# Cached attention with a gated feed-forward branch: who begins the loads of keys and values

## The chip, the core and the metric

The kernel runs on one core of a Trainium2 chip. A core has a matrix engine (TensorE, PE in the profile), a vector engine (VectorE, DVE), a scalar engine (ScalarE, ACT), GpSimd (POOL) and SyncE (SP), which run their own instruction streams and meet at semaphores. Sixteen DMA engines move data between the chip's main memory (HBM) and the on-chip memory (SBUF); transfers are begun by an instruction on one of the engines' queues. The metric is the device time of one execution in microseconds (us), as the median of several runs.

## The reference, cut to what matters

```python
# x [4,1,512]; k_cache, v_cache [4,32,4096,128]; wq [512,4096]; wo [4096,512]
def _A_ref(x, k_cache, v_cache, wq, wo):
    q = (x @ wq).reshape(B, Sq, H, Dh).transpose(0, 2, 1, 3)
    scores = jnp.einsum("bhqd,bhkd->bhqk", q, k_cache) * (Dh ** -0.5)
    p = softmax(scores, axis=-1)
    o = jnp.einsum("bhqk,bhkd->bhqd", p, v_cache)
    return o.transpose(0, 2, 1, 3).reshape(B, Sq, H * Dh) @ wo

def _B_ref(x, w_gate, w_up, w_down):
    return (gelu(x @ w_gate) * (x @ w_up)) @ w_down

g = sigmoid((x * gate_w).sum(-1, keepdims=True))
out = g * _A_ref(...) + (1 - g) * _B_ref(...)
```

Everything is float32. The two caches hold 268 MB each, read once.

## The kernel before, in words

**Tiles.** A tile is four heads of one batch row: 8.39 MB of keys or of values, laid on 128 partitions with 64 KB in a row on each. There are 32 key tiles and 32 value tiles (NT = 32). Keys have two buffers, `K[0]` and `K[1]`, used in turn; values have one, `V`. The weights share these buffers: `wq` is loaded into `V` first, and `w_gate`, `w_up`, `w_down` and `wo` go into the key buffers at the end.

**The start.** SP begins `wq`, `x` and `gate_w` (L143 to L147), then key tiles 0 and 1 (L148, L149), all in one queue. GpSimd makes the identity matrix `ident` (L151, L153). TensorE turns `x` (L170), multiplies it with `wq` (L200) and turns the result (L212; its last mark is `wq_done`, after which `V` is free); ScalarE and TensorE spread the first query into `QB` (L225 to L231).

**One tile.** `keys(s)` on VectorE waits for the key tile (`sem_k[s]`) and for the query, multiplies in place (L293) and sums (L294); then it counts up `k_free`, which says that the key buffer may be filled again, and finds the maxima (L296 to L298). ScalarE takes exponentials (`weights`, L308). TensorE sums the weights (`totals`, L234), waits for the value tile (`sem_v`), multiplies (`values`, L241), and turns the result (`turn`, L246), whose first instruction gives the mark `at_tile[i]`: `V` is free again. VectorE divides (L301, L302).

**The order of the loads** (L338 to L344): SP waits for `wq_done` and begins value tile 0. Then, for i from 0 to 29, it waits for `k_free` to reach i + 1 and begins key tile i + 2, waits for `at_tile[i]` and begins value tile i + 1. Waits and loads stand in SP's program order, and each load (`load`, L132) is a `dma_start` on SP's queue that adds 16 to its semaphore when it has landed. The engines that use a tile subtract the 16 again (`take`, L122).

**The end** (L346 to L383): when key tile 30 is worked off, SP begins `w_gate` and `w_up` into `K[0]`, then value tile 31 (waiting for `at_tile[30]`), then, when key tile 31 is worked off, `w_down` and the first part of `wo` into `K[1]`. The products with `w_gate` and `w_up` (L280) run on TensorE in front of tile 31's; from them VectorE and ScalarE make `hT` (L362 to L375), and after it SP begins the rest of `wo` in five pieces. `project` (L401) adds the rows of `w_down` and `wo`; the last four rows of `wo` go through L456, and the result `res` (L460) is stored.

Of the kernel before, what the change touches and what calls it, by code (L numbers as in the profile page):

```python
# [34 lines left out]
def tile_gated_mix(ctx: ExitStack, tc: tile.TileContext, x, kc, vc, wq, wo, w_gate, w_up, w_down, gate_w, out):  # L35
    nc = tc.nc
# [10 lines left out]
    NT = NG * B  # L47
# [33 lines left out]
    K = [kv.tile([P, TW], F32, name=f"k{s}") for s in range(2)]  # L81
    V = kv.tile([P, TW], F32, name="v")
# [20 lines left out]
    tot, quo = bank[2][:, :HT], bank[3][:, :HT]  # L103

    stored, parting = (ctx.enter_context(nc.semaphore(name)) for name in ("stored", "parting"))
    counters = []

    def semaphore(name):
        counters.append(ctx.enter_context(nc.semaphore(name)))
        return counters[-1]  # L110

    ctx.enter_context(tc.tile_critical(sync_engine=mybir.EngineType.SP))
    SP = Line(nc.sync, None)
# [3 lines left out]
    PL = Line(nc.gpsimd, semaphore("pl"))  # L117
    a_to_p, d_to_p, p_to_a, d_to_a, p_to_d, a_to_d, d_to_d = (
        semaphore(name) for name in ("a_to_p", "d_to_p", "p_to_a", "d_to_a", "p_to_d", "a_to_d", "d_to_d"))
    k_free = semaphore("k_free")  # L120
# [4 lines left out]
    sem_k = [semaphore(f"sem_k{s}") for s in range(2)]  # L125
    sem_v = semaphore("sem_v")

    def heads(src, i):
        g, b = divmod(i, B)
        return src[b, HT * g:HT * g + HT].rearrange("h (p r) d -> (h p) (r d)", p=PH)  # L130

    def load(dst, src, sem=None, name=None):  # L132
        sem = sem or semaphore(name)
        nc.sync.dma_start(dst, src).then_inc(sem, 16)  # L134
        return sem, 16

    def load_k(i):
        load(K[i % 2], heads(kc, i), sem_k[i % 2])

    def load_v(i):  # L140
        load(V, heads(vc, i), sem_v)

    got_q = load(V, wq.rearrange("(p c) n -> p (c n)", c=KC), name="got_q")  # L143
    x_sb = o[:B]
    got_x = load(x_sb, x.rearrange("b s d -> (b s) d"), name="got_x")
    gw = gs[:B]
    got_g = load(gw, gate_w.rearrange("(o n) -> o n", o=1).to_broadcast([B, DM]), name="got_g")  # L147
    load_k(0)  # L148
    load_k(1)  # L149

    p0 = PL.do(nc.gpsimd.memset(ident, 0.0))  # L151
    PL.wait(p0)
    have_ident = PL.do(nc.gpsimd.affine_select(out=ident, in_=ident, compare_op=OP.not_equal, fill=1.0, base=0,  # L153
                                               pattern=[[-1, P]], channel_multiplier=1))
    DV.do(nc.vector.memset(ones, 1.0))
    DV.do(nc.vector.memset(PM, 0.0))
    have_zeros = DV.do(nc.vector.memset(RS, 0.0))
# [51 lines left out]
    for s in range(2):  # L209
# [3 lines left out]
        wq_done = PE.do(u)  # L213
# [43 lines left out]
    L1 = NT - 1  # L257
    PE.wait(have_QX, have_picks, have_zeros)
    at_tile = [(PE.sem, PE.n + i + 1) for i in range(NT)]
    f, down = K[0], K[1]  # L260
# [74 lines left out]
            beside(s, i)  # L335
    beside(0, None)

    SP.wait(wq_done)  # L338
    load_v(0)
    for i in range(NT - 2):  # L340
        SP.wait((k_free, i + 1))
        load_k(i + 2)
        SP.wait(at_tile[i])
        load_v(i + 1)  # L344

    wo_rows = wo.rearrange("(p i) n -> p (i n)", i=WR)  # L346
    SP.wait((k_free, NT - 1))
    for s, a in enumerate((w_gate, w_up)):
        load(f[:, s * KC * F:(s + 1) * KC * F], a.rearrange("(p c) n -> p (c n)", c=KC), sem_up[s])
    SP.wait(at_tile[L1 - 1])  # L350
    load_v(L1)
    SP.wait((k_free, NT))
    got_down = load(down[:, :DR * DM], w_down.rearrange("(p i) n -> p (i n)", i=DR), name="got_down")
    got_wo = [load(down[:, (DR + r0) * DM:(DR + r1) * DM], wo_rows[:, r0 * DM:r1 * DM], name=f"got_wo{r0}")
              for r0, r1 in ((0, W0), (W0, W1))]

# [88 lines left out]
    i = W2  # L445
# [15 lines left out]
    load(out.rearrange("b s (c n) -> c (b s) n", c=4), res[::8], stored)  # L461
    nc.sync.sem_inc(parting, 1)
    nc.gpsimd.wait_ge(parting, 1).then_inc(parting, -1)
    nc.gpsimd.sem_clear(range(counters[0].num, counters[-1].num + 1))
    nc.sync.wait_ge(stored, 16).then_inc(stored, -16)

# [21 lines left out]
```

## Time and profile before

| | |
|---|---|
| median of 3 runs | 1311.45 us (1311.39 to 1311.8) |
| profiled execution: span from first to last instruction | 1309.8 us |
| outside the span, against the median | 1.65 us |
| busy share of VectorE | 87% |
| busy share of TensorE, ScalarE, GpSimd | 30%, 8%, below 1% |
| HBM read | 564.67 MB, 431 GB/s over the span |

A time line row reads: start in us, duration in us, engine, line, operation, tile written and read, and in brackets the idle time before with what ended it. A row of costly groups has, after the count, the busy time in us, the mean of one in ns, and the idle time before them. A row of DMA issues has the tile, the queue, the count, the KB of one where they are few, and the median time from issue to landing in us. A row of a DMA queue has its packets, its MB and the share of the time of 16 engines. A row of the busy time by stretch has start and end, length, the busy us of PE, weight loads, DVE, ACT and POOL, the granted clock of TensorE, the DMA share and GB/s.

### The profile page before, as it was taken

How to read it: one execution, taken by the hardware profiler on the slowest of the kernel's cores; microseconds unless marked ns; L12 is line 12 of the kernel's file. 1: busy time of each engine (PE TensorE's matmuls, PEld its weight loads, DVE VectorE, ACT ScalarE, POOL GpSimd, SP SyncE). 2: the span in 40 equal slices, each digit the busy share in tenths (PEclk: the TensorE clock that was granted, in tenths of full speed). 3: DMA queues.
4: the chain of work that ended last, by engine and by line, in shares of the span. 5: the costliest groups of instructions: out<-in, count | busy, mean ns of one | idle time of the engine just before them, and what ended most of it. 6: DMA issues, size and time to landing. Idle time of an engine off the chain costs nothing. (4 is left out here: it accounts for less than half of the span.)

```text
span 1309.8 us, 6988 instructions
## 1 busy us (share of the span) xinstructions
PE 387.9 (30%) x2708; PEld 134.1 (10%) x2708; DVE 1144.5 (87%) x266; ACT 108.6 (8%) x360; POOL 0.7 (0%) x6
## 2 busy tenths in 40 slices
PE   2133123333213333312333321233231133332157
PEld 0010001111001111000111100011010011100012
DVE  1799999999999989989999998999999998999950
ACT  0000000000000000000000000000000000000010
POOL 0000000000000000000000000000000000000000
PEclk9665566666556666656666655666655666665578
DMA  9999999999999999999999999999999999999998
GB/s 417 416 445 421 444 432 432 444 422 442 424 442 422 444 438 426 444 424 442 422 442 428 438 442 424 442 424 442 422 444 432 432 444 422 442 424 442 423 433 352
DMA packets 10842, 564.76 MB, mean 431 GB/s; under 512 B 1212, under 2 KB 1228, under 8 KB 1620
## 3 DMA queue, kind: packets, MB, share of 16 engines
q1 hardware_dynamic: 10836, 564.69, 99.6%
q8 instruction: 3, 0.05, 0.0%
q14 instruction: 3, 0.02, 0.0%
HBM read 564.67 MB, written 0.01 MB: 431 GB/s over the span
## 5 line engine op out<-in xcount | busy, mean ns | idle before, releaser
L293 DVE TENSOR_TENSOR k<-k,QB 128x16384 f32<-128x16384 f32 x32 | 551.2, 17225 | 57.8 <-DVEq L123 57.8
L294 DVE TENSOR_REDUCE SC<-k 128x128 f32<-128x16384 f32 x32 | 551.0, 17220 | 4.7
L241 PE MATMUL bank<-v,PM 128*16 128x512 f32 x2048 | 292.8, 736 | 507.6 <-PEq L123 507.6
L241 PEld LDWEIGHTS bank<-v,PM 128*16 128x16 f32 x2048 | 68.8, 113 | 704.9 <-issue 704.8
L234 PE MATMUL bank<-RS,ones 128*128 128x4 f32 x64 | 17.9, 350 | 348.4 <-PEq L123 348.4
L308 ACT ACTIVATE PM<-SC,nm 32x128 f32<-32x128 f32 x128 | 66.0, 516 | 249.4 <-ACTq L123 247.9
L321 ACT ACTIVATE o<-bank 128x512 f32<-128x512 f32 x31 | 18.5, 597 | 811.7 <-ACTq L123 811.7
L234 PEld LDWEIGHTS bank<-RS,ones 128*128 128x128 f32 x64 | 16.0, 311 | 353.5 <-issue 353.5
L246 PE MATMUL bank<-pick,o 128*128 128x4 f32 x256 | 32.8, 252 | 28.8 <-PEq L123 28.8
L246 PEld LDWEIGHTS bank<-pick,o 128*128 128x128 f32 x256 | 31.0, 191 | 57.3 <-issue 57.3
L301 DVE RECIPROCAL ri<-bank 128x4 f32<-128x4 f32 x32 | 5.8, 183 | 22.5 <-DVEq L123 22.5
L308 ACT ACTIVATION_READ_ACCUMULATOR PM<-SC,nm 32x1 f32 x128 | 25.1, 196 | 0.0
L174 DVE COPY xT<-bank 128x32 f32<-128x32 f32 x4 | 0.5, 184 | 21.2 <-PE bank L170 21.2
L228 PE MATMUL bank<-ident,QX 128*128 128x128 f32 x66 | 15.5, 316 | 1.7 <-ACT QX L225 1.6
L296 DVE TENSOR_REDUCE m<-SC 128x1 f32<-128x128 f32 x32 | 9.2, 287 | 7.6 <-DVEq L123 7.6
L231 ACT ACTIVATE QB<-bank 128x128 f32<-128x128 f32 x32 | 8.9, 277 | 50.3 <-ACTq L123 49.7
L302 DVE TENSOR_TENSOR OT<-bank,ri 128x4 f32 (+1 forms) x32 | 5.2, 161 | 7.5 <-DVEq L123 7.2
L297 DVE STREAM_TRANSPOSE mt<-m 128x32 f32<-128x32 f32 x32 | 6.8, 211 | 4.7
L228 PEld LDWEIGHTS bank<-ident,QX 128*128 128x128 f32 x66 | 10.0, 191 | 3.2 <-issue 1.9
L460 DVE COPY res<-bank 128x128 f32<-128x128 f32 x1 | 0.3, 292 | 11.4 <-PE bank L456 11.4
L298 DVE TENSOR_REDUCE nm<-mt 128x1 f32<-128x32 f32 x32 | 6.0, 186 | 4.8 <-DVEq L123 2.1
L225 ACT ACTIVATE QX<-QT 128x128 f32 (+1 forms) x32 | 9.8, 308 | 2.4 <-DVE QT L216 1.6
(57 smaller groups left out, 61.1 us busy)
## 6 DMA issues: line engine op xcount, KB each, us to landing
k<-in_B_w_gate SPq DMA_DIRECT2D x1, 3584.0 KB, 31.3
k<-in_B_w_up SPq DMA_DIRECT2D x1, 3584.0 KB, 39.4
k<-in_B_w_down SPq DMA_DIRECT2D x1, 3584.0 KB, 29.0
k<-in_A_wo SPq DMA_DIRECT2D x1, 2560.0 KB, 34.7
k<-in_A_wo SPq DMA_DIRECT2D x1, 2048.0 KB, 39.1
k<-in_A_wo SPq DMA_DIRECT2D x1, 1536.0 KB, 33.6
k<-in_A_wo SPq DMA_DIRECT2D x1, 1024.0 KB, 35.7
k<-in_A_k_cache SPq DMA_DIRECT2D x32, 42.1
```

What stands on the lines that cost most here:

```text
L225: return nc.scalar.activation(QX, tile_of(QT, pair, s)[:, :, None].to_broadcast([P, HT, PH]), AF.Copy)
L228: return nc.tensor.matmul(qp[:, :D], QX.rearrange("p h k -> p (h k)"), ident, start=True, stop=True)
L231: nc.scalar.activation(QB[s], qp[:, :D], AF.Copy, scale=scale).then_inc(a_to_d, 1)
L234: return nc.tensor.matmul(tot, ones, RS, start=True, stop=True)
L241: t = nc.tensor.matmul(po[32 * c:32 * c + M], p[:, j * M:(j + 1) * M], V[:, j * RJ * D:(j + 1) * RJ * D], start=j < 4, stop=j >= n - 4)
L246: return [nc.tensor.matmul(quo, o[:, j * D:(j + 1) * D], pick[:, j, :], start=j == 0, stop=j == RJ - 1) for j in range(RJ)]
L293: then(nc.vector.tensor_tensor(k, k, QB[s][:, None, :].to_broadcast([P, R, D]), op=OP.mult))
L294: then(nc.vector.tensor_reduce(SC[s], k, axis=AX.X, op=OP.add))
L296: then(nc.vector.tensor_reduce(m1, SC[s], axis=AX.X, op=OP.max))
L297: then(nc.vector.transpose(mt, m1.to_broadcast([P, 32])))
L308: t = nc.scalar.activation(PM[q, :, h], SC[s][q, :], AF.Exp, bias=NM[s][q, :], scale=1.0, accum_out=RS[q, h:h + 1])
L321: nc.scalar.activation(o, po, AF.Copy).then_inc(a_to_p, 1)
```

## The change

The 64 loads of key and value tiles are begun by GpSimd, in the same order and behind the same waits as on SP before. Key tiles 0 and 1 follow the two instructions that make `ident`. The loads count on three new semaphores, `soft[0]` and `soft[1]` for the key buffers and `soft[2]` for values, which only count up. SP waits for each landing in turn (`pass_on`) and adds 16 to the old semaphore, so that the engines that use the tiles are as before. `w_gate`, `w_up`, `w_down`, `wo`, `wq`, `x`, `gate_w` and the store stay on SP; in its program they now stand behind the pass-ons: `w_gate` behind that of value tile 30, the first part of `wo` behind that of value tile 31. At the end GpSimd resets and clears the three semaphores.

```diff
+    soft = [ctx.enter_context(nc.semaphore(f"soft{s}")) for s in range(3)]
...
     def load_k(i):
-        load(K[i % 2], heads(kc, i), sem_k[i % 2])
+        nc.gpsimd.dma_start(K[i % 2], heads(kc, i)).then_inc(soft[i % 2], 16)
 
     def load_v(i):
-        load(V, heads(vc, i), sem_v)
+        nc.gpsimd.dma_start(V, heads(vc, i)).then_inc(soft[2], 16)
...
-    load_k(0)
-    load_k(1)
 
     p0 = PL.do(nc.gpsimd.memset(ident, 0.0))
     PL.wait(p0)
     have_ident = PL.do(nc.gpsimd.affine_select(out=ident, in_=ident, ...
+    load_k(0)
+    load_k(1)
...
-    SP.wait(wq_done)
+    PL.wait(wq_done)
     load_v(0)
     for i in range(NT - 2):
-        SP.wait((k_free, i + 1))
+        PL.wait((k_free, i + 1))
         load_k(i + 2)
-        SP.wait(at_tile[i])
+        PL.wait(at_tile[i])
         load_v(i + 1)
+
+    def pass_on(of, n, to):
+        nc.sync.wait_ge(soft[of], 16 * n)
+        nc.sync.sem_inc(to, 16)
+
+    pass_on(0, 1, sem_k[0])
+    pass_on(1, 1, sem_k[1])
+    for i in range(NT - 1):
+        pass_on(2, i + 1, sem_v)
+        if i + 2 < NT:
+            pass_on(i % 2, (i + 2) // 2 + 1, sem_k[i % 2])
 
     wo_rows = wo.rearrange("(p i) n -> p (i n)", i=WR)
     SP.wait((k_free, NT - 1))
     for s, a in enumerate((w_gate, w_up)):
         load(f[:, s * KC * F:(s + 1) * KC * F], a.rearrange("(p c) n -> p (c n)", c=KC), sem_up[s])
-    SP.wait(at_tile[L1 - 1])
+    PL.wait(at_tile[L1 - 1])
     load_v(L1)
-    SP.wait((k_free, NT))
+    SP.wait(at_tile[L1 - 1], (k_free, NT))
     got_down = load(down[:, :DR * DM], w_down.rearrange("(p i) n -> p (i n)", i=DR), name="got_down")
+    pass_on(2, NT, sem_v)
     got_wo = [load(down[:, (DR + r0) * DM:(DR + r1) * DM], wo_rows[:, r0 * DM:r1 * DM], name=f"got_wo{r0}")
               for r0, r1 in ((0, W0), (W0, W1))]
...
     nc.sync.sem_inc(parting, 1)
     nc.gpsimd.wait_ge(parting, 1).then_inc(parting, -1)
+    nc.gpsimd.dma_reset(range(soft[0].num, soft[2].num + 1))
+    nc.gpsimd.sem_clear(range(soft[0].num, soft[2].num + 1))
     nc.gpsimd.sem_clear(range(counters[0].num, counters[-1].num + 1))
```

## The prediction

> **What bounds the kernel now.** I read the page first, for who is busy.
>
> ```profile
> span 1309.8 us, 6988 instructions
> q1 hardware_dynamic: 10836, 564.69, 99.6%
> L293 DVE TENSOR_TENSOR k<-k,QB 128x16384 f32<-128x16384 f32 x32 | 551.2, 17225 | 57.8 <-DVEq L123 57.8
> L294 DVE TENSOR_REDUCE SC<-k 128x128 f32<-128x16384 f32 x32 | 551.0, 17220 | 4.7
> k<-in_A_k_cache SPq DMA_DIRECT2D x32, 42.1
> v<-in_A_v_cache SPq DMA_DIRECT2D x32, 28.1
> ```
>
> SyncE's DMA queue holds the 16 DMA engines for 99.6% of the span. VectorE needs 17.23 + 17.22 us and some small work per tile. Next the busy time by stretch, for the rate:
>
> ```profile
> 100.00:700.00 600.00, 166.93 (x1142) 58.35 (x1142) 563.77 (x113) 50.94 (x173) 0.00 (x0) 0.61 1.00 434
> ```
>
> The DMA share is 1.00 at 434 GB/s, so one tile of 8.39 MB takes 19.33 us, and a key tile with its value tile 38.66 us, over VectorE's 34.45 us of large work. The kernel is as long as its bytes. Whatever leaves the DMA engines without work is added to the time, and whatever only delays an engine is not, unless it empties the queue. So the question is where the change empties the queue. The profiled span is 1309.8 us; the median of the runs, 1311.45 us, has 1.65 us around it. I add the difference to the median. A measurement of this kernel can tell about 0.2%, 2.6 us.
>
> **The middle of the kernel.** This is the time line of one tile:
>
> ```profile
> 660.54 17.22 DVE L294 TENSOR_REDUCE SC<-k 128x128 f32<-128x16384 f32 x1
> 672.34 0.33 SPq L134 DMA_DIRECT2D v<-in_A_v_cache  x1
> 677.93 0.33 SPq L134 DMA_DIRECT2D k<-in_A_k_cache  x1
> 681.74 17.23 DVE L293 TENSOR_TENSOR k<-k,QB 128x16384 f32<-128x16384 f32 x1 [2.22 <-DVEq L123]
> ```
>
> The 62 loads behind the first two move from SP's queue to GpSimd's with their two waits each (k_free, at_tile); GpSimd has no other work there. Their order stays, so on the new queue they still go one behind the other. How long a load takes that finds nothing ahead of it is shown by wq, the first of all (its row is below): 22.0 us, that is 19.33 and 2.7 us of start and landing. A value tile is issued 28.1 us ahead of its landing, a key tile 42.1: they lie 6.1 and 20.1 us in the queue. Up to 6 us of slower issue per load is hidden there by the transfers in front; without that cover it would cost its full length. SP's pass-on puts one wait and one increment between landing and consumer. No row shows the pair alone; the nearest is one DMA issue on SP, 0.33 us, so 0 to 0.33 us, and I take 0.1. Nothing else is queued on SP that these waits could hold, until the last tiles. VectorE takes a key tile that much later, and has 38.66 - 34.45 us to spare less some 2 us of small work; TensorE's end of a value tile comes 6 us early. So the middle costs nothing.
>
> **The start.** The rows from wq to value tile 1:
>
> ```profile
> 0.96 0.40 SPq L134 DMA_DIRECT2D v<-in_A_wq  x1
> 1.38 0.29 POOL L153 TENSOR_SCALAR_AFFINE_SELECT ident<-ident 128x128 f32<-128x128 f32 x1 [0.23 <-POOL ident L151]
> 2.12 0.93 SPq L134 DMA_DIRECT2D k<-in_A_k_cache  x2
> 23.05 0.61 PE L170 MATMUL bank<-ident,o 4*128 4x4 f32 x4 [23.05 <-DMA o<-in_A_x]
> 37.95 0.33 SPq L134 DMA_DIRECT2D v<-in_A_v_cache  x1
> 39.30 0.28 ACT L231 ACTIVATE QB<-bank 128x128 f32<-128x128 f32 x1 [0.58 <-PE bank L228]
> 42.54 17.23 DVE L293 TENSOR_TENSOR k<-k,QB 128x16384 f32<-128x16384 f32 x1 [4.16 <-DVEq L123]
> 77.31 0.33 SPq L134 DMA_DIRECT2D k<-in_A_k_cache  x1
> 91.78 0.33 SPq L134 DMA_DIRECT2D v<-in_A_v_cache  x1
> ```
>
> Before, key tile 0 stands behind wq in one queue. After, GpSimd begins it at about 1.7 us, when ident is made, 0.7 us behind wq, on a queue of its own. The two then share the engines. What a queue is made of is seen in the packet counts of two stretches:
>
> ```profile
> DMA packets 4469, 260.19 MB, mean 434 GB/s; under 512 B 498, under 2 KB 498, under 8 KB 498
> q1 hardware_dynamic: 560, 1.79, 44.2%
> ```
>
> The second is of 1300 to 1310 us and is used further below. These are the landings of wq, key tile 2 and value tile 0, the last number being us from issue:
>
> ```profile
> v<-in_A_wq SPq DMA_DIRECT2D x1, 22.0
> k<-in_A_k_cache SPq DMA_DIRECT2D x1, 24.7
> v<-in_A_v_cache SPq DMA_DIRECT2D x1, 43.2
> ```
>
> The first stretch (100 to 700 us) gives 3971 large packets of 260 MB, 65.5 KB each: a tile is 128 packets, 8 on each engine, 2.42 us apiece. If the engines take turns packet by packet, 7 of key tile 0's packets go between wq's 8, and wq lands 7 x 2.42 = 16.9 us later: 22.96 becomes 39.9. The ends of this are 0 (wq goes first) and 38.7 (16 packets, both key tiles go first). I take turns, as no row prefers a queue. [...] No row shows two busy queues.
>
> x stands behind wq, so TensorE's first step (23.05) moves with it, and the chain to the first query, 23.05 to 39.58, follows: 56.5. VectorE began at 42.54 because key tile 0 was the last to arrive; now the query is, and it begins at 56.6, 14.1 us later. Key tile 2 needs the buffer that VectorE leaves after that: issued at 77.31, now at 91.4. Value tile 0 is issued later too (37.95 + 16.9 = 54.9) but in time: wq and two key tiles fill the engines to about 62. It lands at 37.95 + 43.2 = 81.15 as before. So from about 81 the engines have nothing until key tile 2. On an empty queue it takes 22.0 us and lands at 113.4, against 77.31 + 24.7 = 102.0: **11.4 us** lost. To this comes what GpSimd's issue takes longer than SP's on an empty queue. No row shows it; between nothing and one more start and landing (2.7 us) I take one more SP issue, **0.4 us**. [...]
>
> It is lost once. VectorE then runs 14 us late, works off key tiles 0 and 1 by about 127 (twice 34.45 us and the small work) and frees the second buffer while value tile 1 (113 to 133) is under way, which was issued at 91.78 + 14.1 = 105.9. From there each tile gives VectorE 2 to 3 us back.
>
> **The end.** SP's program order now decides something:
>
> ```profile
> 1214.15 0.33 SPq L134 DMA_DIRECT2D v<-in_A_v_cache  x1
> 1218.86 0.33 SPq L134 DMA_DIRECT2D k<-in_B_w_gate  x1
> 1252.27 0.33 SPq L134 DMA_DIRECT2D v<-in_A_v_cache  x1
> 1257.43 0.33 SPq L134 DMA_DIRECT2D k<-in_B_w_down  x1
> 1278.15 9.75 PE L241 MATMUL bank<-v,PM 128*16 128x512 f32 x64 [10.38 <-PEq L123]
> 1294.75 4.56 PE L401 MATMUL bank<-k,ow 128*4 128x512 f32 x36 [0.38 <-DVE ow L427]
> v<-in_A_v_cache SPq DMA_DIRECT2D x1, 27.6
> k<-in_B_w_gate SPq DMA_DIRECT2D x1, 3584.0 KB, 31.3
> k<-in_B_w_up SPq DMA_DIRECT2D x1, 3584.0 KB, 39.4
> 1269.58 36.42 DMA k<-in_A_wo
> 1306.54 0.29 DVE res L460
> ```
>
> The gate load was issued at 1218.86 and lay behind value tile 30, which landed at 1214.15 + 27.6 = 1241.75. Now its issue stands on SP behind the pass-on of that very tile, so it goes out at 1241.9 onto empty engines (value tile 31 needs value tile 30 computed). 3.67 MB take 8.46 us, with start and landing 11.1: it lands at 1253.0 instead of 1250.2, **2.8 us** lost. Bounds: 0, if it were queued as before, and 2.8 plus the 0.33 of a slower pass-on.
>
> What comes behind it shares the engines between two queues: value tile 31 (issued about 10.5 us after tile 30 lands) with the rest of up, then down. Packets of up and down are 28.7 KB, 1.06 us each. At 1253 six of up's 16 per engine are left; in turns with 65.5 KB packets up ends about 1274.5 and tile 31 about 1281.5, with down still going to 1287.8, so SP's last pass-on releases wo in time and the engines stay full. Tile 31 is then 3.7 us later than before (1278), and the chain from it (16.6 us to 1294.75, then 28 rows of wo at 4.56/18 us, 7.1) would end at about 1305.5; wo's bytes, which end the kernel (36.42 us of the chain of waits, then the result at 1306.54), come at about 1308.8 and still end last. If the queues share by bytes instead, tile 31 comes near 1288.5, and that chain ends last, about 7 us later than before. So the end is +2.8, from 0 to +8.
>
> ```profile
> SPq L465 <- SPq L465: 1.1, 1, 1.1
> ```
>
> GpSimd's reset and clear of the new semaphores stand beside SP's 1.1 us wait for the output's landing. [...]
>
> **Sum:** 11.4 + 0.4 + 2.8 + 0.3 = 14.9 us on 1311.45, that is **1326.4 us**.
>
> **The rivals.**
>
> *wq goes first* (0.13): GpSimd's first packets come so late, or are served so rarely, that wq is hardly delayed. The query has 3.0 us in hand (39.58 to 42.54), and key tile 2, issued 3.8 us before value tile 0 lands, some 2.5 (3.8 less half of the 2.7): a delay of 5.5 us, two packets, costs nothing. It decides from GpSimd's first packet being five packets, 12 us, behind wq's, and gives 1311.45 + 3.1 = 1314.6 us. [...]
>
> *GpSimd's loads go first* (0.12): both key tiles pass ahead of wq. wq lands at 61.6, the query at 78.3, key tile 2 is issued at 113.1 and lands at 135.1, 33 us late: 1348 us.
>
> *The transfers themselves are slower, or blocked* (0.2). The second packet row gives 0.442 x 16 x 10 us = 70.7 us of engine time for 1.79 MB, which at 27.1 GB/s are 66.0: the other 4.7 over 560 packets are 8.4 ns a packet. If GpSimd's queue cuts 65.5 KB rows to 16 KB, a tile takes 1.0% more, 13 us in all; at 4 KB 5.2%, 64 us. With small packets the start would be cheaper. So 1325 to 1390 us. [...]
>
> *The new queue is faster* (0.05). The loads would have to make good 15 us over 64, 0.23 us of 19.33 each: from 439 GB/s on, the change is not slower, and at 445 GB/s (18.85 us) it gives 1296 us. For it: the last packets of one queue and the first of another might overlap their 8.4 ns. Against: that is 8 x 8.4 ns, 0.07 us a tile.
>
> **How the numbers follow.** The forecast has 0.5 and reaches from 1321 to 1334 (issue 0 to 2.7, end 0 to +8). With the two rivals beside it the range is 1314 to 1351; it leaves out the upper half of the slow transfers and the faster queue, 0.15. Slower by over 0.2% is everything but the last rival and a part of the first: 0.91; the same 0.05; faster 0.04.
>
> **What would show it.** Right: key tile 0 and wq both land near 40 us; the first L293 begins near 56.6; the DMA row shows a hole of some 11 us between 80 and 92 and a smaller one where value tile 30 lands, and 434 GB/s between. Wrong: a first L293 near 43 (wq went first) or 78 (last); packets per tile other than 128, or a rate other than 434 GB/s in the middle; holes repeated tile by tile; a gate load that still overlaps value tile 30.

## The result, and the profile after

The changed kernel takes 1333.55 us (median of 4 runs, 1333.37 to 1334.06) against 1311.43 us: 1.0169 times as long, 95% interval 1.0157 to 1.0181. That is 22.1 us slower; the forecast was 14.9 us slower (1326.4 us, range 1314 to 1351). The profiled execution has a span of 1332.3 us, 22.5 more than before.

The page of the changed kernel, its DMA busy tenths and GB/s in 40 slices, and its queues:

```profile
span 1332.3 us, 7055 instructions
DMA  9959999999999999999999999999999999999898
GB/s 409 410 220 410 439 439 439 429 427 437 441 439 425 431 437 439 439 421 437 437 439 437 419 441 437 439 433 423 439 439 439 429 427 439 439 437 429 376 449 346
q0 software_dynamic: 9216, 536.88, 93.1%
q1 hardware_dynamic: 1620, 27.81, 5.0%
```

GpSimd's queue (q0) now moves the 64 tiles, SyncE's (q1) the rest. The third slice has half the rate of the others, and a later one (376) has some less. The busy time by stretch puts the two holes beside the middle:

```profile
83.00:98.00 15.00, 0.00 (x0) 0.00 (x0) 14.61 (x3) 0.00 (x0) 0.40 (x1) 0.50 0.00 0
130.00:1230.00 1100.00, 318.70 (x2182) 110.42 (x2186) 1022.83 (x204) 93.14 (x316) 30.06 (x57) 0.62 1.00 434
1259.50:1261.50 2.00, 0.47 (x4) 0.18 (x8) 2.00 (x1) 0.00 (x0) 0.00 (x0) 0.50 0.00 0
```

For 15 us at the start and 2 us near the end the DMA engines move nothing. Between them they move 434 GB/s, the rate of the kernel before. This is how the first hole comes about, in the time line of the changed kernel:

```profile
0.97 0.40 SPq L135 DMA_DIRECT2D v<-in_A_wq  x1
1.91 1.19 POOL L139 DMA_DIRECT2D k<-in_A_k_cache  x2 [0.22 <-issue]
42.68 0.61 PE L171 MATMUL bank<-ident,o 4*128 4x4 f32 x4 [42.68 <-DMA o<-in_A_x]
47.51 0.68 DVE L179 TENSOR_TENSOR gs<-gs,o 4x512 f32<-4x512 f32 x1 [3.71 <-DMA gs<-in_gate_w]
49.65 8.79 PE L201 MATMUL bank<-v,xT 128*32 128x512 f32 x64
61.05 0.53 POOL L142 DMA_DIRECT2D v<-in_A_v_cache  x1 [57.95 <-PE bank L213]
62.14 0.28 ACT L232 ACTIVATE QB<-bank 128x128 f32<-128x128 f32 x1 [0.58 <-PE bank L229]
62.57 17.23 DVE L294 TENSOR_TENSOR k<-k,QB 128x16384 f32<-128x16384 f32 x1 [1.35 <-DVEq L124]
97.60 0.53 POOL L139 DMA_DIRECT2D k<-in_A_k_cache  x1 [36.03 <-DVEq L296]
```

and in its DMA issues, the landings of wq and of key tile 2:

```profile
v<-in_A_wq SPq DMA_DIRECT2D x1, 39.0
k<-in_A_k_cache POOLq DMA_DIRECT2D x1, 23.6
```

wq lands at 39.97 instead of 22.96, x at 42.68 instead of 23.05, and gate_w, which came out together with wq and x before, at 47.5. The first query is ready at 62.42 instead of 39.58, VectorE begins at 62.57 instead of 42.54, and key tile 2 is issued at 97.60 and lands at 121.2 instead of 102.0: 19.2 us late.

That shift then stays. VectorE's starts of three tiles, before (the first two rows, line 293) and after (line 294):

```profile
488.62 17.23 DVE L293 TENSOR_TENSOR k<-k,QB 128x16384 f32<-128x16384 f32 x1 [2.36 <-DVEq L123]
1222.66 17.23 DVE L293 TENSOR_TENSOR k<-k,QB 128x16384 f32<-128x16384 f32 x1 [2.21 <-DVEq L123]
```

```profile
507.81 17.22 DVE L294 TENSOR_TENSOR k<-k,QB 128x16384 f32<-128x16384 f32 x1 [2.36 <-DVEq L124]
1241.84 17.23 DVE L294 TENSOR_TENSOR k<-k,QB 128x16384 f32<-128x16384 f32 x1 [2.21 <-DVEq L124]
```

It is 19.19 us at the one and 19.18 us at the other, 19 tiles later: 38 loads by GpSimd have added nothing. The end of the changed kernel, from its time line:

```profile
1260.95 0.36 SPq L135 DMA_DIRECT2D k<-in_B_w_gate  x1
1303.87 3.58 SPq L135 DMA_DIRECT2D k<-in_A_wo  x7
```

from its DMA issues:

```profile
k<-in_B_w_gate SPq DMA_DIRECT2D x1, 3584.0 KB, 11.2
```

and from its chain of waits:

```profile
1271.53 32.23 DMA v<-in_A_v_cache
1307.03 21.45 DMA k<-in_A_wo
1329.02 0.29 DVE res L473
```

The gate load goes out when value tile 30 has landed and been passed on, onto empty engines: 11.2 us from issue to landing, where it was 31.3 in the queue. It lands at 1272.15 instead of 1250.2, 22.0 us late, so 2.8 us more than the 19.2. Value tile 31 takes 32.23 us beside up and down; wo follows without a hole and still ends the kernel. The result is copied at 1329.02 instead of 1306.54: 22.5 us, that is 19.2 + 2.8 + 0.5.

### The profile page after: what moved, and what is told of

The parts are those of the page before. It is cut to its first block, busy times and chain, and to the rows that moved or that the text cites. A ratio compares the mean times of both kernels' runs of the same rounds, so it can differ in the third digit from the quotient of the medians.

```text
span 1332.3 us, 7055 instructions
## 1 busy us (share of the span) xinstructions
PE 386.6 (29%) x2708; PEld 134.1 (10%) x2708; DVE 1144.6 (86%) x266; ACT 108.6 (8%) x360; POOL 34.6 (3%) x70
## 3 DMA queue, kind: packets, MB, share of 16 engines
q0 software_dynamic: 9216, 536.88, 93.1%
## 5 line engine op out<-in xcount | busy, mean ns | idle before, releaser
L142 POOL DMA_DIRECT2D v<-in_A_v_cache x32 | 16.9, 527 | 988.4 <-PE bank L247 930.4
L139 POOL DMA_DIRECT2D k<-in_A_k_cache x32 | 17.0, 532 | 248.1 <-DVEq L296 247.9
L281 PE MATMUL bank<-k,xT 128*32 128x448 f32 x64 | 7.8, 636 | 17.7 <-PEq L124 17.7
## 6 DMA issues: line engine op xcount, KB each, us to landing
k<-in_B_w_gate SPq DMA_DIRECT2D x1, 3584.0 KB, 11.2
k<-in_B_w_up SPq DMA_DIRECT2D x1, 3584.0 KB, 31.3
```

Of the source, the lines that this page charges most:

```text
L139: nc.gpsimd.dma_start(K[i % 2], heads(kc, i)).then_inc(soft[i % 2], 16)
L142: nc.gpsimd.dma_start(V, heads(vc, i)).then_inc(soft[2], 16)
```

## The experiments

The theory after the result: nothing is lost in the loads themselves; a second queue makes wq, x and gate_w take turns with the key tiles (19 us), and SyncE's program order makes a hole behind value tile 30 (3 us). The main rival: loads from GpSimd are slower, 22 us over 64. Each time below stands against runs of the kernel before on the same chip (1311.36 to 1311.57 us).

**1. Key tiles 0 and 1 back on SyncE, the other 62 loads on GpSimd.**

```diff
+    load(K[0], heads(kc, 0), sem_k[0])     # on SyncE, behind gate_w
+    load(K[1], heads(kc, 1), sem_k[1])
...
-    load_k(0)                              # on GpSimd
-    load_k(1)
...
-    pass_on(0, 1, sem_k[0])
-    pass_on(1, 1, sem_k[1])
...
-            pass_on(i % 2, (i + 2) // 2 + 1, sem_k[i % 2])
+            pass_on(i % 2, (i + 2) // 2, sem_k[i % 2])
```

> The changed kernel, but key tiles 0 and 1 are begun by SyncE behind wq, x and gate_w, as before; the other 62 loads stay on GpSimd. Theory (the start is lost because wq, x and gate_w take turns with two key tiles of a second queue, the rest at the hole behind value tile 30): the start is as before, key tile 2 lands near 102 us, and 1311.4 + 2.9 + 0.5 = about 1315 us. Rival (each load from GpSimd is a little slower, 22 us over 64, or 0.34 us each): 62 of 64 stay, so about 1332 us.

Measured: 1316.62 us, 1.0036 (1.0023 to 1.005). 62 of the 64 loads cost 5.1 us, so the rival falls. It is 1.7 us more than expected. The time line shows where they come from:

```profile
37.40 0.67 POOL L142 DMA_DIRECT2D v<-in_A_v_cache  x1 [35.71 <-PE bank L213]
44.96 17.23 DVE L294 TENSOR_TENSOR k<-k,QB 128x16384 f32<-128x16384 f32 x1 [7.41 <-DVEq L124]
80.02 0.53 POOL L139 DMA_DIRECT2D k<-in_A_k_cache  x1 [41.95 <-DVEq L296]
490.50 17.23 DVE L294 TENSOR_TENSOR k<-k,QB 128x16384 f32<-128x16384 f32 x1 [2.36 <-DVEq L124]
```

Value tile 0, on GpSimd's queue, now gets in ahead of key tile 0's last packets on SyncE's. By the packet records of the trace (the start, length and size of each packet) these are the 4-byte packets that report the landing, on 6 of the 16 engines. VectorE begins at 44.96 instead of 42.54, 2.42 us later, the time of one packet. Key tile 2 is issued 2.7 us late, and from the middle on 1.9 us of it stay (490.50 against 488.62).

**2. The other way round: the kernel before, with only key tiles 0 and 1 on GpSimd.**

```diff
-    load_k(0)
-    load_k(1)
...
+    for i in range(2):                     # behind ident
+        nc.gpsimd.dma_start(K[i], heads(kc, i)).then_inc(soft[i], 16)
...
+    pass_on(0, 1, sem_k[0])
     SP.wait(wq_done)
     load_v(0)
+    pass_on(1, 1, sem_k[1])
...
```

> The kernel before, with only key tiles 0 and 1 begun by GpSimd, and SyncE passing on these two landings; everything else as before. Theory: the whole loss of the start, key tile 2 lands near 121 us against 102, so 1311.4 + 19 = about 1330.5 us. Rival (cost per load): 2 of 64 loads, about 1312 us.

Measured: 1331.13 us, 1.0148 (1.0132 to 1.0163), 19.6 us. Two loads make nearly the whole loss.

**3. The same with ScalarE in GpSimd's place.**

```diff
-    load_k(0)
-    load_k(1)
+    for i in range(2):
+        nc.scalar.dma_start(K[i], heads(kc, i)).then_inc(sem_k[i], 16)
```

> The kernel before, with only key tiles 0 and 1 begun by ScalarE's queue, and no load by GpSimd at all. Theory (any second queue takes turns with wq): the two key tiles start about 5 us earlier than GpSimd's did (2 us against 7.6), so wq loses about two more turns of 2.42 us; VectorE begins near 67 us and the time is about 1331 + 5 = 1335 us. Rival (it is GpSimd's way of loading that hurts): 1311 to 1313 us.

Measured: 1335.01 us, 1.0181 (1.0166 to 1.0197), 23.5 us.

```profile
0.91 0.90 ACTq L149 DMA_DIRECT2D k<-in_A_k_cache  x2
46.91 0.61 PE L170 MATMUL bank<-ident,o 4*128 4x4 f32 x4 [46.91 <-DMA o<-in_A_x]
66.92 17.23 DVE L293 TENSOR_TENSOR k<-k,QB 128x16384 f32<-128x16384 f32 x1 [1.35 <-DVEq L123]
```

With no load on GpSimd the same happens, and more of it, as the key tiles come first: x at 46.91, VectorE at 66.92. By the packet records the engines take turns with ScalarE's queue as with GpSimd's, one 65.5 KB packet each. It is the second queue, not GpSimd.

**4. The changed kernel with x and gate_w begun ahead of wq.**

```diff
-    got_q = load(V, wq..., name="got_q")
     x_sb = o[:B]
     got_x = load(x_sb, ...)
     gw = gs[:B]
     got_g = load(gw, ...)
+    got_q = load(V, wq..., name="got_q")
```

> The changed kernel, but SyncE begins x and gate_w ahead of wq instead of behind it. Theory (each small packet behind wq waits for a whole turn of 2.42 us of the key tiles: x came 2.7 us and gate_w 7.5 us behind wq): x and gate_w land within 5 us, TensorE begins the product with wq as soon as wq lands, near 40 us instead of 49.65, VectorE begins near 52.9 instead of 62.6, and the time is about 1333.5 - 10 = 1323.5 us. Rival (only wq's own bytes count, the small loads come out with it): within 3 us of 1333.5.

Measured: 1326.09 us, 1.0107 (1.0091 to 1.0122): 7.5 us less than the changed kernel, where 10 were expected and at most 3 by the rival.

```profile
40.60 9.76 PE L201 MATMUL bank<-v,xT 128*32 128x512 f32 x64 [34.69 <-DMA v<-in_A_wq]
54.48 17.23 DVE L294 TENSOR_TENSOR k<-k,QB 128x16384 f32<-128x16384 f32 x1 [1.35 <-DVEq L124]
```

The product with wq begins at 40.60, released by wq, instead of 49.65. So two 8 KB loads behind wq cost 9 us of the start, 8 of which reach VectorE (62.57 to 54.48). The other one goes into the product itself, 9.76 us here and 8.79 in the changed kernel; no run shows why.

**5. The changed kernel with all loads of the end on GpSimd, in the old order.**

```diff
-    SP.wait((k_free, NT - 1))
+    PL.wait((k_free, NT - 1))
     for s, a in enumerate((w_gate, w_up)):
-        load(..., sem_up[s])
+        soft_load(..., 3 + s)              # nc.gpsimd.dma_start(...).then_inc(soft[3 + s], 16)
     PL.wait(at_tile[L1 - 1])
     load_v(L1)
...                                         # w_down and wo in the same way
+    pass_on(3, 1, sem_up[0])
+    pass_on(4, 1, sem_up[1])
     pass_on(2, NT, sem_v)
```

> The changed kernel, but w_gate, w_up, w_down and all of wo are begun by GpSimd as well, in the order of the kernel before and behind the same waits, so that no load of the end stands behind a pass-on; SyncE passes on w_gate, w_up and value tile 31, the others are waited for directly. Theory (the end loses 2.9 us in the hole behind value tile 30 and 0.5 by what follows): the hole is gone and the time is about 1330 us. Rival (the end's loss lies in the store, the reset of semaphores or elsewhere): 1333.5 us as before.

Measured: 1331.2 us, 1.0149 (1.0133 to 1.0164), 2.3 us less than the changed kernel and 1.2 more than expected. The gate load lies in the queue again:

```profile
k<-in_B_w_gate POOLq DMA_DIRECT2D x1, 3584.0 KB, 31.0
```

In its trace the result is copied at 1325.59, 3.4 us earlier than in the changed kernel (0.1 of them from the start): the loss of the end is gone up to there. But from the copy to the end of the span it takes 3.7 us, where the kernel before and the changed kernel take 3.3. The four runs that reset 13 semaphores (5, 6, 8 and 9) all have 3.7 there, the other runs 3.3.

**6. Both repairs.** The edits of runs 1 and 5 together:

```diff
+    load(K[0], heads(kc, 0), sem_k[0])     # and K[1]: on SyncE, as in run 1
...
+    PL.wait((k_free, NT - 1))              # w_gate to wo on GpSimd, as in run 5
```

> Both repairs: key tiles 0 and 1 begun by SyncE as before, and the loads of the end begun by GpSimd in the old order. 62 tile loads and the weights of the end still come from GpSimd, with SyncE's pass-ons. Theory (GpSimd's loads in the middle cost nothing): 1311.4 us within 1 us. Rival (a small cost per load or per pass-on that the two holes cover up): each 0.05 us per load shows as 3 us, so 1314 us or more.

Measured: 1313.5 us (11 runs), 1.0014 (1.0005 to 1.0023). The large terms are gone, yet 2.0 us stay, outside of what was expected, and less than the rival's 3. The first row is of the kernel before:

```profile
78.58 17.22 DVE L293 TENSOR_TENSOR k<-k,QB 128x16384 f32<-128x16384 f32 x1 [0.23 <-DVEq L123]
81.19 17.23 DVE L294 TENSOR_TENSOR k<-k,QB 128x16384 f32<-128x16384 f32 x1 [2.85 <-DVEq L124]
490.54 17.23 DVE L294 TENSOR_TENSOR k<-k,QB 128x16384 f32<-128x16384 f32 x1 [2.36 <-DVEq L124]
1224.57 17.23 DVE L294 TENSOR_TENSOR k<-k,QB 128x16384 f32<-128x16384 f32 x1 [2.22 <-DVEq L124]
```

Against before (488.62 and 1222.66) the shift is 1.92 and 1.91 us. So they too are lost at the start and not by the loads of the middle. Tile 1 begins 2.6 us late (81.19 against 78.58): its keys, on SyncE, share the engines with value tile 0, on GpSimd. Runs 8 and 9 take this up.

**7. The changed kernel, with GpSimd waiting for wq before key tiles 0 and 1.**

```diff
+    PL.wait(got_q)
     load_k(0)
     load_k(1)
```

> The changed kernel, but GpSimd waits for wq to land before it begins key tiles 0 and 1, so no turns are taken; the engines stand idle from wq's end until GpSimd's first load starts. Theory: x and wq land at 23 us as before; the idle stretch is 1.3 us if GpSimd's first load starts as its later ones do, or 5.7 us if the 5.7 us seen at the start of the changed kernel belong to the first load wherever it stands; key tile 0 lands at 44 to 48 us, and the time is 1311.4 + 3.4 + 1.5 to 6 = 1316 to 1321 us. Rival (loads from GpSimd cost by themselves): 1330 us or more.

Measured: 1318.21 us, 1.0052 (1.0037 to 1.0068). One wait takes 15.3 us off the changed kernel, though it leaves the engines without work for some 2 us.

```profile
23.09 1.19 POOL L139 DMA_DIRECT2D k<-in_A_k_cache  x2 [21.40 <-DMA v<-in_A_wq]
45.43 17.23 DVE L295 TENSOR_TENSOR k<-k,QB 128x16384 f32<-128x16384 f32 x1 [6.64 <-DVEq L124]
```

By the packet records the first packet of key tile 0 starts at 24.48, 1.4 us behind the issue; in the changed kernel it was 5.7 (1.91 to 7.58). So 5.7 us are not the price of GpSimd's first load: there, two packets of wq on each engine went first.

**8. Both repairs, and value tile 0 on SyncE as well.**

```diff
-    PL.wait(wq_done)
-    load_v(0)
+    SP.wait(wq_done)
+    load(V, heads(vc, 0), sem_v)
```

> The kernel with both repairs, and value tile 0 begun by SyncE too, so that at the start one queue holds wq, both key tiles and value tile 0, in the old order; the other 61 tile loads and the weights of the end come from GpSimd. Theory (the 2.0 us that both repairs left over come from key tile 1 on SyncE's queue and value tile 0 on GpSimd's taking turns between 42 and 81 us, since VectorE's start of tile 1 moved from 78.58 to 81.19 and the shift then stays as it is): tile 1 starts near 78.6 again and the time is 1311.5 us within 0.5. Rival (the 2 us are the price of GpSimd's loads or of the pass-ons): about 1313.4 us as before.

Measured: 1313.03 us (11 runs), 1.0013 (1.0004 to 1.0022). The theory holds for VectorE's start of tile 1 and not for the time, which is nearly the rival's; run 9 decides between the rest of the start and the price of all loads.

```profile
77.69 0.68 POOL L139 DMA_DIRECT2D k<-in_A_k_cache  x1 [76.00 <-DVEq L296]
78.68 17.23 DVE L294 TENSOR_TENSOR k<-k,QB 128x16384 f32<-128x16384 f32 x1 [0.23 <-DVEq L124]
490.06 17.23 DVE L294 TENSOR_TENSOR k<-k,QB 128x16384 f32<-128x16384 f32 x1 [2.36 <-DVEq L124]
1224.09 17.23 DVE L294 TENSOR_TENSOR k<-k,QB 128x16384 f32<-128x16384 f32 x1 [2.22 <-DVEq L124]
```

Tile 1 begins at 78.68 as before, and the shift in the middle is still 1.44 and 1.43 us. The shift of tile 1 was 0.1 us, so the 1.4 us come in behind it. Key tile 2 is the next load, and GpSimd's first here.

**9. Key tile 2 on SyncE too; 60 tile loads and the end stay on GpSimd.**

```diff
+    SP.wait((k_free, 1))
+    load(K[0], heads(kc, 2), sem_k[0])     # GpSimd's loop begins with value tile 1
```

> As the run before it, with key tile 2 begun by SyncE as well; from value tile 1 on all tile loads, and the weights of the end, come from GpSimd (60 tile loads). Key tile 2 is issued only some 2.5 us before the engines run out of work; every later load has 6 us or more. Theory (the last 1.5 us come from key tile 2 alone, because GpSimd's load is ready later than SyncE's, and the loads that lie long in the queue cost nothing): 1311.6 us within 0.5, and VectorE's starts as before at every tile. Rival (the switch of queues, or GpSimd's loads in general, cost the 1.5 us wherever the first of them stands): about 1313 us again.

Measured: 1311.91 us (11 runs), 1.0004 (0.9995 to 1.0013): no difference that can be told.

```profile
488.55 17.23 DVE L294 TENSOR_TENSOR k<-k,QB 128x16384 f32<-128x16384 f32 x1 [2.36 <-DVEq L124]
1222.58 17.23 DVE L294 TENSOR_TENSOR k<-k,QB 128x16384 f32<-128x16384 f32 x1 [2.21 <-DVEq L124]
1306.45 0.29 DVE L482 COPY res<-bank 128x128 f32<-128x128 f32 x1 [11.86 <-PE bank L478]
```

Every quoted start, and the result (1306.45 against 1306.54), lies within 0.1 us of the kernel before. Sixty tile loads and the weights of the end on GpSimd, with their pass-ons on SyncE, cost nothing that can be told. The half microsecond left in the median is within the noise; in the trace 0.4 us lie behind the result, in the longer stretch named in run 5. No version beat the kernel before, whose queue holds the DMA engines for 99.6% of the span.

## Why the prediction was right, and which term was too small

**What bounds the kernel** was read rightly: only holes in the DMA engines' work counted. The middle cost 0, as forecast (run 9), though VectorE began its first tiles 20 us late.

**The start** was the right mechanism with too small a size: 11.4 + 0.4 were forecast, 19.2 measured. wq's landing was forecast to the tenth (39.9; 39.97), in part by luck. The forecast puts seven packets of key tile 0 between wq's eight. By the packet records two of wq's packets go ahead of GpSimd's first on each engine, so only six come between wq's eight; the seventh goes ahead of the 4-byte packet that reports wq's landing (38.97 to 39.59 over the engines), which the forecast does not have.

The step that failed is "x stands behind wq, so TensorE's first step moves with it, and the chain to the first query follows". It counted turns for wq's packets alone. x came 2.7 us behind wq and gate_w another 4.8, one turn of 2.42 us and two, where before they came out together with it. By the packet records x's data and the packets that report its landing start in one turn (from 41.4), gate_w's data in the next (from 43.9) and its reports in one more (from 46.4). TensorE's order puts the small product that needs gate_w ahead of the product with wq, so the chain from x to the query grew from 16.5 to 19.7 us. Together the query came at 62.42 instead of the forecast 56.5, 5.9 us. Run 4 shows this: with the two loads ahead of wq, 7.5 us go. That is more than 5.9, as the steps on x and gate_w then lie ahead of wq's landing too.

The rest, 1.5 us, lies at key tile 2. GpSimd began it 35.03 us after VectorE's start, where SyncE in run 2 took 34.77: 0.3 us. It landed 23.6 us behind its issue where 22.4 was taken: 1.2 us. Most of that is not GpSimd's, as SyncE's key tile 2 in run 2, on empty engines as well, took 23.4. Value tile 0 was not in time either: GpSimd issued it at 61.05, not 54.9, and its first packet starts at 62.28, when all earlier ones have ended (at 61.4). This gap cost nothing, as key tile 2 had to wait for VectorE until 97.6.

"GpSimd's loads go first" came out neither for GpSimd nor for ScalarE; "wq goes first" did not either. The engines took turns: by the packet records of the changed kernel, from 7.58 us on, single packets of 65.5 KB from the two queues alternate until wq's last, each of 2.42 us. The delay in run 1 is as long as one such packet, 2.42 us.

**The end** was right: 2.8 forecast for the hole behind value tile 30, 2.8 measured in the profile, and gone in run 5. Of what comes behind it, the queues shared by packets (from 1275 on one of 65.5 KB and one of 28.7 KB in turn, by the packet records): value tile 31 landed 43 us behind tile 30, where 39.8 was forecast and 46.8 for sharing by bytes. wo ended last, as forecast. No run shows the 0.3 us taken for the reset of the semaphores: from the copy of the result to the end of the span it is 3.3 us before and after. The 0.5 us that came on top of 19.2 + 2.8 lie ahead of the result and are gone in run 5, so they belong to the order of the loads at the end; no run divides them further.

**The range.** The measured time lies inside the forecast's own stretch, 1321 to 1334, by half a microsecond. What brought it up there, the turns of the small loads, is not among the terms that make the stretch (issue 0 to 2.7, end 0 to +8), so that it holds is luck in part. Its low end does not follow from its terms, either: 1311.45 + 11.4 + 0.3 are 1323.2. And where the working for the end has "six of up's 16", the 16 packets on an engine are those of gate and up together, eight each.

**The rival of slower or blocked transfers** falls, and that of a faster queue with it: packets of 65.5 KB on GpSimd's queue (8192 of the 9216 by the packet records, the others 4 bytes), 434 GB/s and starts that do not drift.

**What stays open:** why key tile 2 from GpSimd loses 1.4 us in run 8, where SyncE's in run 9, issued 0.4 us earlier, loses nothing. By the packet records its first packets start 0.4 us, on average, after value tile 0's last ones have ended, and the first two on each engine take 3.02 and 2.67 us on average; SyncE's in run 9 start without a gap and take 2.50 and 2.42. That makes about 1.1 of the 1.4 us. The time from issue to first packet alone does not explain it: on empty engines GpSimd's first packet started 1.24 us behind the issue (97.60 to 98.84 in the changed kernel; SyncE's 0.98 in run 2), and here it had 2.3 us. Why the first packets are later and longer was not tried.

## What to carry to other kernels

Before a load is moved to another queue, ask what stood behind what in the old one: here the order in one queue gave the first load, and the chain behind it, the whole of the DMA engines. Where the engines were full, a second queue brought no bandwidth (434 GB/s with both) and delayed what was urgent; one wait for the urgent load (run 7) gave back 15 of 22 us. Loads that lay in the queue for 6 us or more could be begun by GpSimd as well as by SyncE (run 9). Look at the few that start on empty engines or nearly so, and at other work that now stands behind a wait in program order.

## What the runs showed that was not expected

- Small loads behind a large one waited for whole turns of the second queue: x (8 KB) came 2.7 us and gate_w (8 KB) 7.5 us behind wq. Even the 4-byte packets that report a landing waited their turn: gate_w's came 2.5 us behind its data (43.9 to 46.4). Begun ahead of wq they were in time, and the product with wq then began at 40.60 instead of 49.65.
- ScalarE's two loads, issued at 0.91 us ahead of wq, cost 23.5 us; GpSimd's, issued at 1.9 us behind it, 19.6. By the packet records ScalarE's first packets run ahead of wq's, GpSimd's behind two of wq's on each engine. wq lands at 42.5 with ScalarE and at 39.9 with GpSimd (run 2), about one turn apart, and x and gate_w fall behind by more.
